# Linear attention with a feed-forward layer on one core: two loads moved to GpSimd's queue with a cast, the second weight in two pieces, and a new order of the work

## The chip, the cores and the metric

The kernel runs on one core of one Trainium2 chip. A core has five engines that run side by side, each through its own list of instructions: TensorE (PE, matrix products; PEld is its weight load), VectorE (DVE), ScalarE (ACT), GpSimd (POOL) and SyncE (SP), which here only issues transfers. Sixteen DMA engines move data between the main memory and the on-chip memory SBUF; the results of matmuls lie in the eight banks of PSUM. The metric is the device time of one execution in microseconds, as the median of several runs.

## The reference

For each of 4 batches and 8 heads, over 768 steps of 48 channels, a state of 48 x 48 is decayed and updated, and read by q:

```python
f = 1.0 / (1.0 + np.exp(-f_logit))
for t in range(S):
    state = f[:, :, t, :, None] * state + np.einsum('bhd,bhe->bhde', k[:, :, t], v[:, :, t])
    y[:, :, t] = np.einsum('bhd,bhde->bhe', q[:, :, t], state)
```

The heads of y are laid side by side, which gives 3072 tokens of 384 channels. A feed-forward layer follows:

```python
h = x @ w_in                       # 384 -> 2048
g = h * (1.0 / (1.0 + np.exp(-h)))
return g @ w_out                   # 2048 -> 384
```

All inputs and the output are float32; w_in and w_out have 3.1 MB each.

## The kernel before

The 768 steps of each batch are cut into six chunks of 128. A chunk of one batch, with its eight heads, is a "unit of work"; two of them form a pair, and there are twelve pairs (lines 19 to 32). Pairs 0 to 3 have the form T: they hold the chunks 0 and 1 of one batch, and the 128 partitions hold two neighbouring steps each, so that one load of 384 KB brings the f (or k, q, v) of both chunks in runs of 384 bytes. Pairs 4 to 11 have the form N: the same chunk of two batches, mostly in two loads of 192 KB.

A step of the work has a short name and the pair's number, and for most kinds the half of the pair (0 or 1):

- `f`, `k`, `q`, `v`: the loads (lines 224 to 241), all on SP's queue before the change.
- `E`, `L`: ACT turns f_logit into the log of the decay (exp, then ln). `cs`: PE sums it over time by a product with a triangular matrix. `ia`, `a`: ACT takes the exponential of the sum, with both signs; `al`: the decay over a whole half.
- `ki`, `qg`: k and q times these factors, on DVE or POOL (line 341). `tq`: PE transposes both, `qkc` copies them out of PSUM; for later pairs a transposing transfer `qkD` does both.
- `sc`: the scores of one half against the other operand, `at`: DVE masks them. `sc` of a T pair reads the transposed tiles of both halves.
- `vb`: v is cast to bfloat16 by ACT, DVE or POOL (line 343).
- `y`, `yi`: the output from the scores and from the state before. `d`, `sd`, `su`: the update of the state.
- `yc`, `yT`, `xc` (or `yD`): the output is cast and transposed into the input of the feed-forward layer.
- `wi`, `wo`: the loads of w_in and w_out, issued by POOL and cast to bfloat16 by the transfer (lines 209 to 219). Before, each comes in four pieces. `wi.n` holds the columns of `mi` blocks 2n and 2n + 1; a piece `wo.n` holds rows of w_out.
- `mi`: one block of 256 of the 2048 hidden channels (line 271). For pairs 0 and 1 it is cut once more by the half of the pair, so that `mi.0.4.1` is pair 0, block 4, half 1, of six matmuls. `si`: the sigmoid-weighted step on ACT (line 276). `mo`: a quarter of the product with w_out (line 306, four matmuls); `mo.P.i.n` uses rows 4n to 4n + 3 of sixteen blocks of rows. `oc`: the copy of the result out of PSUM. `so`: its store.
- `idle.512.n`: n matmuls of 512 columns on a tile of zeros (line 465), whose result nobody reads.

The order is written out by hand, as it were: the string `PLAN` (line 37) is a list of words `step:engine:buffers`. `f.2.0:S:1` is the load of f for pair 2, issued by S (SP), into buffer 1 of its class; A, V, G, P are ACT, DVE, POOL and PE. `SLOTS` (line 34) says how many buffers a class has. The kernel walks through the words (lines 510 to 516) and gives each step to its engine, so that each engine executes its own steps in the order of the words, and waits at a step until its inputs are there and its buffer is free. An engine never skips a step that waits. Ahead of everything else stand the first four loads of the list (line 482), then some constants are built. `count` (line 174) finds into how many pieces a load is cut from the number of words that name it, and `cast` (line 177) holds the pairs whose v is issued by G: such a load goes into a bfloat16 tile `vq` (lines 227 and 228), and `values` (line 199) then reads that tile where it otherwise reads `vb`. The code for this is there before the change; the plan before does not use it.

Two waits are named in the steps of the prediction. `y.0` writes into PSUM buffers that earlier `cs` tiles held, and can start when `ia` and `a` have read them. POOL's steps between the weight loads (`ki.3.0`, `qg.2.1`, `qg.3.0`, `qg.3.1`, `vb.3.0`) wait for loads on SP's queue.

Of the kernel before, what the change touches and what calls it, by code (L numbers as in the profile page):

```python
# [33 lines left out]
SLOTS = dict(f=4, k=6, q=6, v=6, e=2, lf=3, x=5, qk=5, vb=7, qkT=4, qkTT=2, atm=4, yb=3, xT=4, hT=4, sd=2, al=6, ob=6, pb=8, st0=1, st1=1, st2=1, st3=1)  # L34
# [15 lines left out]
mi.1.1.0:P:0 mi.1.4.0:P: qg.3.0:V: mi.1.1.1:P: si.1.4:A: mi.1.6.1:P:4 v.4.1:S:4 si.0.5:A: mi.0.1.1:P:6 mi.1.0.0:P:3 si.1.1:A: mi.1.3.1:P:5 mi.0.0.1:P:  # L50
mi.0.1.0:P: si.0.0:A: mi.1.0.1:P: si.0.3:A: mi.0.7.0:P:0 mi.0.6.1:P:7 mi.1.3.0:P: mi.1.7.0:P:1 si.1.3:A: mi.0.6.0:P: si.0.1:A: mi.1.7.1:P: mi.1.6.0:P:
tq.3.0:P:5 si.1.6:A: mo.0.0.0:P:6 si.1.7:A: si.0.6:A: tq.3.1:P:4 si.0.4:A: mi.0.7.1:P: qkc.3.1:V:1 mo.0.0.1:P: si.1.0:A: qkc.3.0:V: si.0.7:A:
mo.0.1.0:P:1 vb.2.1:G:4 vb.3.1:A:5 mo.0.1.1:P: vb.3.0:A:6 vb.2.0:G:2 sc.3.1:P:7,2 sc.3.0:P:4,3 at.3.1.0:V:2 f.5.0:S:1 mo.0.1.2:P: at.3.0.1:V:3
mo.1.1.0:P:5 q.5.1:S:4 at.3.0.0:V: mo.1.1.1:P: mo.1.1.2:P: E.4.0:A:0 v.4.0:S: mo.1.1.3:P: mo.0.1.3:P: v.8.1:S:5 mo.0.0.2:P: oc.0.1:V:0 k.4.1:S:4
at.3.1.1:V: y.2:P:0,7 oc.1.1:V:1 v.5.0:S:0 d.2:P:3,4 yc.2.0:A:0 d.3:P:1,2 su.2.0:V:0 so.1.1:G: y.3:P:5,0 yc.3.0:V:2 yi.2.1:P: yT.2.0:P:3 yc.2.1:A:1
mo.0.0.3:P: su.1.1:G:0 L.4.0:A:1 mo.1.0.0:P:5 oc.0.0:V:2 q.6.0:S:5 xc.2.0:A:2 su.3.0:V:0 yT.2.1:P:7 so.0.0:G: yT.3.0:P:6 cs.4.1:P:3 sd.2.1:V:1
mo.1.0.1:P: a.4.1:A:3 q.4.1:S:0 xc.2.1:V: E.5.0:A:1 cs.4.0:P:1 mi.2.7:P:4 k.5.1:S:5 ia.4.1:A:0 ia.4.0:A:2 mi.2.5:P:7 ki.4.1:G:3 k.4.0:S: al.4.0:A:4
al.4.1:A:5 L.5.0:A:2 mo.1.0.2:P: su.2.1:G:0 a.4.0:A:4 yi.3.1:P: mi.2.1:P:3 yc.3.1:V:0 q.4.0:S: mi.2.6:P:1 f.6.0:S:2 yT.3.1:P:0 mo.1.0.3:P: xc.3.1:V:3
xc.3.0:V: v.5.1:S: sd.3.1:V:0 mi.2.3:P:0 qg.4.1:V: mi.3.3:P:6 si.2.3:A:2 si.2.1:A: mi.2.4:P:2 si.2.7:A: mi.2.0:P:0 si.2.6:A: mi.3.5:P:3 si.2.0:A:
qkD.4.1:S:0 si.2.5:A: mi.3.1:P:4 si.3.5:A:3 mi.3.2:P:1 si.3.3:A: mi.3.6:P:0 vb.4.1:A:3 k.5.0:S: mi.2.2:P:7 si.3.6:A: q.5.0:S: si.2.4:A: vb.5.1:G:0  # L60
mo.2.0.0:P:3 f.7.0:S:3 si.2.2:A: mo.2.1.0:P:6 si.3.1:A: mi.3.4:P:0 si.3.2:A: v.7.0:S:1 mi.3.7:P:2 si.3.4:A: mi.3.0:P:7 k.6.1:S:0 mo.2.0.1:P: si.3.0:A:
# [48 lines left out]
def kernel(  # L110
# [436 lines left out]
```

## Time and profile before

| | |
|---|---|
| median of 3 runs | 181.59 us (181.53 to 183.5) |
| the profiled execution | 182.17 us, span 180.3 us |
| PE busy | 171.2 us, 95% of the span |
| PE weight load busy | 129.3 us, 72% |
| ACT busy | 129.0 us, 72% |
| DVE busy | 82.5 us, 46% |
| POOL busy | 63.4 us, 35% |
| SP's queue | 25.60 MB, 71.2% of the DMA engines' time |
| POOL's queue | 6.00 MB, 16.1% |
| mean granted clock of PE | 0.991 |

The span is the part of the execution that the profile covers, from the first instruction to the last; the execution's own time has some 1.9 us around it. Busy time of PE includes the `idle` matmuls, 8.3 us for 25 of them. The queue q1 is SP's, q0 is POOL's. A row of the timeline gives the start, the duration, the engine, the line and the operation, its output and input, how many instructions are merged, and in brackets how long the engine had been idle and what ended that.

### The profile page before, as it was taken

The numbers are of one execution on the slowest core, as the hardware profiler recorded it, in microseconds if no ns is written. First come the engines' busy times: TensorE is split into PE (matmuls) and PEld (weight loads), VectorE is DVE, ScalarE is ACT, GpSimd is POOL, SyncE is SP. The second block draws the span as 40 slices with busy tenths as digits, with TensorE's granted clock in tenths as the row PEclk, the third lists the DMA queues.
The fourth block names the chain that finished last, engine by engine and source line by source line (L and its number), as shares of the span: only waits on it lengthen the run. The fifth ranks groups of instructions, "written<-read, shape, count | busy, mean of one in ns | idle before, by whom it ended". The sixth has DMA issues, their size and how long they took to land.

```text
span 180.3 us, 4983 instructions
## 1 busy us (share of the span) xinstructions
PE 171.2 (95%) x2045; PEld 129.3 (72%) x2045; DVE 82.5 (46%) x170; ACT 129.0 (72%) x242; POOL 63.4 (35%) x111
## 2 busy tenths in 40 slices
PE   6579999999999999999999999999999999999993
PEld 2237688985778876778679777876776786788692
DVE  6046986124644029775595743167116865200012
ACT  4788787685486989697987579998197895548500
POOL 6027965502344102950488361054034361200001
PEclk9978999999999999999999999999999999999999
DMA  5999999999999999999959898995895889340023
GB/s 117 306 279 279 224 221 206 205 199 192 204 239 190 199 193 194 167 171 197 167 111 160 208 268 128 209 222 128 167 230 134 165 210 171 125 119 0 0 69 110
DMA packets 109366, 31.91 MB, mean 177 GB/s; under 512 B 103536, under 2 KB 108768, under 8 KB 109344
## 3 DMA queue, kind: packets, MB, share of 16 engines
q1 hardware_dynamic: 104464, 25.60, 71.2%
q0 software_dynamic: 4880, 6.00, 16.1%
q8 instruction: 16, 0.26, 0.6%
q14 instruction: 6, 0.05, 0.1%
HBM read 25.17 MB, written 4.72 MB: 166 GB/s over the span
## 4 chain that ended last, share of the span: by engine, by line
PE 77%; DMA 8%; ACT 5%; POOL 4%; DVE 2%; issue 1%; SPq 1%; ACTq 0%
PE pb L306 34%; PE pb L271 31%; DMA w_in_sb<-in_moe_w_in_dram 5%; DMA f<-in_f_logit_dram 3%; PE pb L373 2%; PE pb L385 2%; POOL qk L341 2%; PE pb L389 2%; ACT hT L276 2%; PE pb L348 1%; PE pb L331 1%; POOL w_in_sb L216 1%; PE pb L406 1%; ACT lf L260 1%; DVE ob L187 1%
## 5 line engine op out<-in xcount | busy, mean ns | idle before, releaser
L306 PE MATMUL pb<-w_out_sb,hT 128*128 128x384 bf16 (+1 forms) x416 | 70.5, 314 | 0.0
L271 PE MATMUL pb<-xT,w_in_sb 128*128 128x256 bf16 (+1 forms) x672 | 68.5, 257 | 0.2
L276 ACT ACTIVATE hT<-pb 128x512 bf16<-128x512 f32 x96 | 51.0, 607 | 19.2 <-PE pb L271 18.9
L271 PEld LDWEIGHTS <-w_in_sb 128*128 128x128 bf16 x672 | 56.7, 97 | 7.6 <-DMA w_in_sb<-in_moe_w_in_dram 0.3
L306 PEld LDWEIGHTS <-hT 128*128 128x128 bf16 x416 | 37.7, 97 | 18.0
L377 DVE TENSOR_TENSOR atm<-pb,triu 128x512 bf16<-128x512 f32 x32 | 20.6, 684 | 28.0 <-PE pb L373 23.9
L336 ACT ACTIVATE x<-pb 128x384 f32<-128x384 f32 x48 | 21.7, 496 | 3.2 <-POOL qk L341 1.9
L420 POOL TENSOR_TENSOR st<-sd,al 48x192 bf16<-48x192 f32 x32 | 17.0, 532 | 15.3 <-PE pb L385 13.7
L187 DVE COPY ob<-pb 128x384 f32<-128x384 f32 (+1 forms) x16 | 8.5, 529 | 27.4 <-PE pb L306 27.4
L513 ACT ACT_TABLE_LOAD x15 | 19.2, 1283 | 0.2
L187 POOL CAST vb<-v 128x384 bf16<-128x384 f32 x12 | 6.5, 552 | 32.4 <-DMA v<-in_v_dram 32.3
L341 POOL TENSOR_TENSOR qk<-k,x 128x384 bf16<-128x384 f32 x9 | 9.3, 1037 | 22.2 <-ACT x L336 13.7
L248 ACT ACTIVATE e<-f 128x768 f32<-128x768 f32 (+1 forms) x13 | 10.4, 799 | 7.2 <-DMA f<-in_f_logit_dram 7.1
L318 POOL DMA_DIRECT2D out_dram<-ob x8 | 4.5, 566 | 28.7 <-DVE ob L187 19.9
L341 POOL TENSOR_TENSOR qk<-q,x 128x384 bf16<-128x384 f32 x10 | 10.3, 1027 | 10.0 <-ACT x L336 5.6
L185 ACT CAST yb<-pb 128x384 bf16<-128x384 f32 x15 | 7.1, 483 | 6.9 <-PE pb L389 3.6
L377 DVE TENSOR_TENSOR atm<-pb,mask 128x512 bf16<-128x512 f32 x16 | 10.2, 683 | 3.3 <-PE pb L369 3.3
L341 DVE TENSOR_TENSOR qk<-k,x 128x384 bf16<-128x384 f32 x15 | 9.8, 667 | 4.1 <-ACT x L336 2.2
L410 DVE TENSOR_TENSOR sd<-pb,st 128x384 f32<-128x384 f32 x16 | 8.8, 552 | 5.9 <-PE pb L406 3.0
L185 ACT COPY ob<-pb 128x384 f32<-128x384 f32 (+1 forms) x10 | 4.6, 458 | 9.3 <-PE pb L306 9.3
L341 DVE TENSOR_TENSOR qk<-q,x 128x384 bf16<-128x384 f32 x14 | 9.3, 667 | 1.7 <-DMA q<-in_q_dram 1.2
L465 PE MATMUL pb<-zero,triu 128*128 128x512 bf16 x25 | 8.3, 471 | 1.4 <-POOL triu masks.py:66 1.4
(71 smaller groups left out, 155.7 us busy)
## 6 DMA issues: line engine op xcount, KB each, us to landing
f<-in_f_logit_dram SPq DMA_DIRECT2D x11, 384.0 KB, 4.9
v<-in_v_dram SPq DMA_DIRECT2D x16, 192.0 KB, 4.0
q<-in_q_dram SPq DMA_DIRECT2D x16, 192.0 KB, 4.4
k<-in_k_dram SPq DMA_DIRECT2D x16, 192.0 KB, 3.9
q<-in_q_dram SPq DMA_DIRECT2D x4, 384.0 KB, 6.1
v<-in_v_dram SPq DMA_DIRECT2D x4, 384.0 KB, 12.3
k<-in_k_dram SPq DMA_DIRECT2D x4, 384.0 KB, 5.6
w_in_sb<-in_moe_w_in_dram POOLq DMA_DIRECT2D x4, 384.0 KB, 9.2
```

The lines of the kernel that those rows point to most:

```text
L185: nc.scalar.copy(dst, src)
L187: ENG[eng].tensor_copy(dst, src)
L248: return nc.scalar.activation(e, at("f", P)[:, j * w:(j + 1) * w], AF.Exp, scale=-1.0)
L271: nc.tensor.matmul(h[:, i, cols], w_in_sb[:, kk, n * 128:(n + 1) * 128], at("xT", P)[:, kk, cols], start=(kk == 0), stop=(kk == KT - 1))
L276: return nc.scalar.activation(at("hT", P)[:, 2 * j:2 * j + 2, :], at("h", P, j).rearrange("p (n c) -> p n c", n=2), AF.Silu)
L306: nc.tensor.matmul(at("o", P, i, *rest[3:])[:, cols], at("hT", P)[:, n, i * C:(i + 1) * C], w_out_sb[:, n, cols], start=(n == 0), stop=(n ...
L336: nc.scalar.activation(at(kind, P, i).rearrange("p h d -> p (h d)"), at("cs", P, i)[:, 0:HD], AF.Exp, scale=1.0 if kind == "ia" else -1.0)
L341: ENG[eng].tensor_mul(at("qk", P, i)[:, j, :, 0:D], heads("qk"[j], P, i), at("ia" if j else "a", P, i))
L377: ENG[eng].tensor_mul(at("atm", P, i)[:, r], at(f"s{r}", P, i).rearrange("p (n c) -> p n c", c=C), mask[:, None, :].to_broadcast([C, NP, C]))
L410: nc.vector.tensor_add(at("sd", P, i), d_ps, prev_state(P, i))
L420: ENG[eng].tensor_mul(at("st", P, i)[lo:lo + D, :, r * D:(r + 1) * D], src[lo:lo + D, :, r * D:(r + 1) * D], al_of(P, i)[lo:lo + D, :, Non ...
L513: nc.scalar.preload_act_table_set(TABLES[mode])
```

## The change

All of it is in `SLOTS` and `PLAN`; no function is edited.

- `v.0.0` and `v.1.0` are issued by G instead of S, with the new class `vq` of two buffers. Each becomes one transfer of 1,024 runs of 384 bytes that casts on its way; `vb.0.0`, `vb.0.1`, `vb.1.0` and `vb.1.1` are gone. The class `v` has five buffers instead of six.
- `wo` has two pieces instead of four, eight blocks of rows each, so that `wo.0` serves `mo.P.i.0` and `mo.P.i.1`, and `wo.1` the other two.
- The first loads on SP's queue are f.2.0, f.0.0, f.0.1, f.1.0 instead of f.0.1, f.0.0, f.2.0, f.1.0: the whole load of f.2 stands ahead of the two halves of f.0.
- The order of all steps is another one, and 76 steps are on another engine. Of stores, for example, POOL issues ten instead of fifteen and SP the others. The order of pairs 2 and 3 in the head is exchanged: k, q and the transposes of pair 3 come first. The `idle` blocks have 23 matmuls in seven places instead of 25 in six.

The number of PE's steps of each kind is the same but for `idle`. The first words of both plans, up to where pair 0's `mi` begin (the two are not aligned with each other):

```diff
-SLOTS = dict(f=4, k=6, q=6, v=6, e=2, lf=3, ..., pb=8, st0=1, st1=1, st2=1, st3=1)
+SLOTS = dict(f=4, k=6, q=6, v=5, e=2, lf=3, ..., pb=8, vq=2, st0=1, st1=1, st2=1, st3=1)
-f.0.1:S:0 f.0.0:S: f.2.0:S:1 f.1.0:S:2 q.0.0:S:0 E.0.1:A:0 E.0.0:A: v.1.0:S:0 L.0.0:A:0 L.0.1:A: E.2.0:A:1 k.0.0:S:0 idle.512.11::0 cs.0.0:P:0
-cs.0.1:P:1 L.2.0:A:1 k.1.0:S:1 a.0.0:A:0 cs.2.0:P:2 a.0.1:A:1 ia.0.0:A:2 q.1.0:S:1 cs.2.1:P:3 E.1.0:A:0 al.0:A:0 L.1.0:A:2 vb.1.0:V:0 f.3.0:S:3
...
+f.2.0:S:0 f.0.0:S:1 f.0.1:S: f.1.0:S:2 k.0.0:S:0 E.2.0:A:0 q.0.0:S:0 E.0.0:A:1 L.2.0:A:0 f.3.0:S:3 E.0.1:A: idle.512.12::0 cs.2.0:P:0 L.0.0:A:1
+L.0.1:A: k.1.0:S:1 idle.512.1::1 cs.0.0:P:1 cs.0.1:P:2 ia.0.0:A:0 q.1.0:S:1 E.1.0:A:0 ki.0.0:G:0 a.0.0:A:1 q.3.0:S:2 al.0:A:0 v.0.0:G:0 ia.0.1:A:2
+qg.0.0:V: L.1.0:A:2 idle.512.3::3 tq.0.0:P:3 k.3.0:S:2 ki.0.1:G:1 a.0.1:A:3 cs.1.0:P:4 cs.1.1:P:5 ia.1.0:A:4 qg.0.1:V: v.1.0:G:1 a.1.0:A:0 q.2.0:S:3
+qkc.0.0:V:0 a.1.1:A:1 idle.512.1::6 tq.0.1:P:6 ia.1.1:A:2 cs.2.1:P:7 E.3.0:A:1 qkc.0.1:V: qg.1.1:G:2 k.2.0:S:3 L.3.0:A:1 sc.0.0:P:1,2 ki.1.1:G:
+sc.0.1:P:4,3 at.0.0.0:V:0 al.2:A:1 al.1:A:2 cs.3.1:P:6 ki.1.0:V:3 wi.2:G: tq.1.1:P:5 at.0.1.1:V:1 wi.1:G: qkc.1.1:A:1 v.2.0:S:0 wi.0:G: qg.1.0:V:
+at.0.1.0:V: a.2.1:A:3 idle.512.3::1 tq.1.0:P:1 ia.3.1:A:1 cs.3.0:P:3 qkc.1.0:V: wi.3:G: al.3:A:3 ia.3.0:A:2 at.0.0.1:V: a.3.0:A:4 v.3.0:S:1 ki.3.0:G:4
+idle.512.2::5 sc.1.1:P:5,4 ia.2.1:A:0 sc.1.0:P:1,3 at.1.1.1:V:2 y.0:P:2,7 at.1.0.1:V:3 a.3.1:A:2 yc.0.0:A:0 at.1.0.0:V: d.0:P:4,6 d.1:P:3,2 qg.2.1:G:0
...
```

After the change the steps of the head stand in this order on three of the engines:

```
SP:   f.2.0 f.0.0 f.0.1 f.1.0 k.0.0 q.0.0 f.3.0 k.1.0 q.1.0 q.3.0 k.3.0 q.2.0 k.2.0 v.2.0 v.3.0 f.4.0
POOL: ki.0.0 v.0.0 ki.0.1 v.1.0 qg.1.1 ki.1.1 wi.2 wi.1 wi.0 wi.3 ki.3.0 qg.2.1 qg.3.0 qg.3.1 su.1.1 wo.0 qg.2.0 su.0.1 vb.3.0 wo.1
PE:   y.0 d.0 d.1 yT.0.0 yi.0.1 y.1 yT.0.1 mi.0.4.0 yi.1.1 tq.3.0 yT.1.0 yT.1.1 mi.0.5.0 mi.0.5.1 mi.0.4.1 mi.1.4.0
      mi.1.2.0 mi.1.3.1 mi.1.3.0 mi.1.5.1 mi.1.2.1 tq.3.1 mi.0.0.1 mi.0.0.0 mi.1.1.1 mi.1.1.0 mi.1.4.1 mi.1.5.0 sc.3.0
      tq.2.1 tq.2.0 mi.0.3.1 mi.0.7.1
```

Before it they stand so:

```
SP:   f.0.1 f.0.0 f.2.0 f.1.0 q.0.0 v.1.0 k.0.0 k.1.0 q.1.0 f.3.0 v.0.0 k.2.0 q.2.0 k.3.0 q.3.0 v.3.0 v.2.0 f.4.0
POOL: ki.0.0 qg.1.1 qg.1.0 wi.1 vb.1.1 wi.2 vb.0.0 ki.2.0 ki.2.1 wi.0 qg.2.0 wi.3 wo.0 wo.1 ki.3.0 wo.2 wo.3 qg.3.1 su.0.1 vb.2.1
```

128 lines of the change are left out of this document (61 added, 67 removed).

## The prediction

> **What bounds the kernel now.** I read the page first, for the span and for which engine is full.
>
> ```profile
> span 180.3 us, 4983 instructions
> PE 171.2 (95%) x2045; PEld 129.3 (72%) x2045; DVE 82.5 (46%) x170; ACT 129.0 (72%) x242; POOL 63.4 (35%) x111
> ```
>
> PE is full, no other engine is. An average over 180 us does not say where PE waits, so the span is cut at the places where its behaviour changes (columns: stretch and its length; busy us and instructions of PE, PEld, DVE, ACT, POOL; clock; DMA share; GB/s).
>
> ```profile
> 0.00:24.90 24.90, 19.50 (x289) 11.84 (x290) 14.75 (x48) 18.39 (x37) 14.15 (x32) 0.93 0.99 239
> 24.90:28.26 3.36, 2.93 (x71) 2.57 (x69) 1.57 (x4) 3.03 (x6) 1.94 (x3) 1.00 1.19 218
> 28.26:32.89 4.63, 4.53 (x83) 4.36 (x79) 3.51 (x6) 2.80 (x5) 1.72 (x3) 1.00 1.21 207
> ...
> 60.00:100.00 40.00, 39.97 (x463) 30.11 (x461) 23.48 (x43) 34.13 (x71) 18.32 (x30) 1.00 0.99 171
> ...
> 140.00:177.40 37.40, 37.34 (x373) 29.31 (x370) 11.76 (x19) 20.96 (x42) 6.56 (x11) 1.00 0.47 106
> ```
>
> From 28.3 us to 177.4 us PE has almost no gap, while the DMA share, about 1 until 100 us, falls to 0.47. Both plans hold the same PE steps (112 `mi`, 104 `mo`, 24 `cs`, 24 `sc`, 20 `y`, 16 `d`, and so on; only the dummy `idle` blocks differ). So an edit that frees ACT, DVE or POOL after 33 us buys nothing, and what counts is how much real PE work is done by a given moment of the head. The timeline shows what the head waits for.
>
> ```profile
> 6.61 0.84 ACT L248 ACTIVATE e<-f 128x768 f32<-128x768 f32 x1 [0.97 <-DMA f<-in_f_logit_dram]
> ...
> 10.20 0.36 DVE L187 CAST vb<-v 128x384 bf16<-128x384 f32 x1 [5.98 <-DMA v<-in_v_dram]
> ...
> 12.32 1.37 POOL L341 TENSOR_TENSOR qk<-k,x 128x384 bf16<-128x384 f32 x1 [8.40 <-DMA k<-in_k_dram]
> ...
> 14.71 1.00 POOL L341 TENSOR_TENSOR qk<-q,x 128x384 bf16<-128x384 f32 x1 [1.02 <-DMA q<-in_q_dram]
> ...
> 16.87 0.95 POOL L216 DMA_DIRECT2D w_in_sb<-in_moe_w_in_dram  x1
> ...
> 32.28 1.30 POOL L341 TENSOR_TENSOR qk<-q,x 128x384 bf16<-128x384 f32 x1 [2.91 <-DMA q<-in_q_dram]
> ...
> 32.89 0.78 PEld L271 LDWEIGHTS <-w_in_sb 128*128 128x128 bf16 x14 [0.27 <-DMA w_in_sb<-in_moe_w_in_dram]
> ```
>
> Nearly every wait is for a load. At 32.89 the last piece of w_in lands, and PE is there 0.27 us early with 17 half-width `mi`, two `tq` and two `sc` of pairs 2 and 3 behind it. That moment is my gauge.
>
> **How the loads share the engines.** A load of f, k, q or v of a T pair is 1,024 runs of 384 B; I call it a unit. DMA traffic in stretches, SP's queue (q1) and POOL's (q0); packets, MB, share of 16 engines: 12 to 16 us; 20 to 24 (two rows); 24 to 28; 28 to 32 (two rows); 36 to 40.
>
> ```profile
> q1 hardware_dynamic: 2850, 1.08, 102.9%
> ...
> q0 software_dynamic: 519, 0.52, 79.7%
> q1 hardware_dynamic: 796, 0.30, 35.0%
> ...
> q0 software_dynamic: 535, 0.53, 78.3%
> ...
> q0 software_dynamic: 626, 0.59, 87.1%
> q1 hardware_dynamic: 631, 0.24, 33.7%
> ...
> q0 software_dynamic: 741, 0.55, 88.1%
> ```
>
> SP alone serves 2,850 packets in 4 us: a unit takes 1.44 us, a packet 64/2850 = 22.5 ns of one of 16 engines. Beside the weights it falls to 796, then 631: 5 to 6.5 us a unit. The queues take turns, 1.5 SP packets to one of POOL's at first, one to one later, and a weight packet is long (0.797 x 64 / 519 = 98 ns for w_in, 0.881 x 64 / 741 = 76 ns for w_out). Hence a load that misses the start of the weights is late by several us. Issues of w_in, of w_out, then k.3 and v.3, each followed by its time to landing (min/median/max):
>
> ```profile
> L216 POOL DMA_DIRECT2D w_in_sb<-in_moe_w_in_dram x4: 779/790/946, 16.9 to 23.2; - x4
> ...
> DMA to landing us min/median/max: 7.5/9.2/9.7
> ...
> L219 POOL DMA_DIRECT2D w_out_sb<-in_moe_w_out_dram x4: 750/762/791, 24.0 to 28.6; - x4
> ...
> DMA to landing us min/median/max: 12.2/14.2/16.0
> ...
> L241 SPq DMA_DIRECT2D k<-in_k_dram x1: 1349/1349/1349, 16.2 to 16.2; - x1
> ...
> DMA to landing us min/median/max: 9.1/9.1/9.1
> ...
> L241 SPq DMA_DIRECT2D v<-in_v_dram x1: 2449/2449/2449, 18.8 to 18.8; - x1
> ...
> DMA to landing us min/median/max: 19.2/19.2/19.2
> ...
> q1 hardware_dynamic: 12876, 4.87, 93.9%
> ...
> q0 software_dynamic: 2, 0.00, 0.1%
> ```
>
> The pieces of w_in land from 24.4 to 32.9, one per 2.8 us; w_out's last at 44.6. The last two rows are the traffic of 0 to 19.8 us: by the first weight packets (2.9 us after their issue) SP has served 12.6 units. So k.3, the 13th, lands at 25.3, q.3, the 14th, at 32.2, v.3, the 15th, at 38.0.
>
> **The change part by part.** *f.2 first.* Two rows for the first two issues (the halves of f.0, together one unit) and one for an Exp of 384 columns:
>
> ```profile
> L241 SPq DMA_DIRECT2D f<-in_f_logit_dram x2: 458/473/488, 0.7 to 1.3; - x2
> ...
> DMA to landing us min/median/max: 2.7/2.8/2.9
> ...
> L336 ACT ACTIVATE x<-pb 128x384 f32<-128x384 f32 x48 | 21.7, 496 | 3.2 <-POOL qk L341 1.9 <-PE pb L331 0.8 <-PE pb L334 0.5
> ```
>
> The first unit lands at 1.3 + 2.9 = 4.2, the second at 6.6, the fifth at 10.2; so f.2 lands at 4.2, f.0's halves at 5.4 and 6.6, k.0 (now the fourth, without v.1 ahead of it) at 9.0 instead of 12.3, q.0 at 10.2. ACT, in its new order, with 0.84 for a whole E or L and 0.5 for a half: E.2 to 5.0, E.0.0 to 5.9, L.2, E.0.1, L.0.0, L.0.1 to 8.3; cs.0.0; ia.0.0 to 9.4 (0.5 us each for `ia` and `a`), E.1, a.0.0, al.0, ia.0.1 to 11.4, L.1, a.0.1, ia.1.0, a.1.0, a.1.1 to 14.2, ia.1.1 to 14.7, E.3, L.3 to 16.4. Behind it stand qkc.1.1 (about 1 us, done at 19.0) and six reads of the `cs` of pairs 2 and 3 to 21.65; the last, ia.2.1, frees the PSUM buffer 7 that y.0 takes. y.0 at 21.7, against about 20 now; then yc.0.0, d.0, d.1, yT.0.0, su.0.0, yi.0.1, y.1, yT.0.1, with 3.6 us of their own durations and hand-overs, and mi.0.4.0 could start at 25.3. The first `mi` now starts at about 25.0: the early f.2 and k.0 buy nothing, since f.0 comes later and ACT has the same work ahead of y.0.
>
> *v.0, v.1 by POOL.* Four casts go; the page prices POOL's:
>
> ```profile
> L187 POOL CAST vb<-v 128x384 bf16<-128x384 f32 x12 | 6.5, 552 | 32.4 <-DMA v<-in_v_dram 32.3
> ...
> L318 POOL DMA_DIRECT2D out_dram<-ob x8: 540/575/587, 106.0 to 176.1; - x8
> ```
>
> They lie beside load waits: worth 0. The issues stand on POOL before ki.0.1 and qg.1.1. ki.0.0 ends at 10.8 (9.4 and the 1.37 of the 12.32 row). A store of 128 runs costs 0.575, a w_out piece of 512 runs 0.762; 1,024 runs by that slope 1.0 us each (bounds 0.6 and 2). POOL: v.0 10.8 to 11.8, ki.0.1, v.1 12.9 to 13.9, qg.1.1 (q.1 lands at 14.6), ki.1.1 to 16.6, then the four w_in issues. They begin no later than now, but q0 is first in, first out, and v stands ahead. No row shows a 384 B run that is cast. Below, a plain packet's 22.5 ns; from the two kinds of weight packets (98 and 76 ns for 2,048 and 1,536 source bytes; 94 by the second q0 row) 26 to 37 ns. I take 30. Then 2 x 64 packets an engine take 3.84 us, and SP's 192 beside them (1.5 to one) 4.3 us: from 13.6 (10.8 + 2.9) to 21.8. In that time SP serves q.3, k.3 and q.2, so q.2 lands near 23; w_in starts **2.0 us later** than at 19.8 and lands from 26.4 to 34.9.
>
> *The order.* PE now: mi.0.4.0 at 26.4, yi.1.1, tq.3.0 (0.5), two yT (0.35), four `mi` of 0.35 (a chain row below: 84 matmuls in 4.86 us) to 29.2; wi.1 is there; five `mi`, tq.3.1 to 31.4; wi.0 at 32.1; six `mi`, sc.3.0, tq.2.1, tq.2.0 to 35.4; mi.0.3.1 to 35.75; wi.3 is there. Before its first use stand 17 half `mi` as before, two more `tq` and one `sc` less: 0.6 us more work. Loss: 35.75 - 32.89 - 0.6 = **2.25 us**.
>
> *w_out in two pieces.* The stretch from there to the first `mo` is 15 `mi`, two `sc` and d.2 (6.3 us): 42.0. wo.0 is issued by POOL at about 28 (behind qg.2.1 at 23 and three steps of 1 us), so it follows w_in without a gap and lands 5.9 us (half of 44.6 - 32.9) behind it: 40.8, hidden by 1.2. wo.1 stands on POOL behind vb.3.0, which waits for v.3; v.3 lands at about 40.8, when wo.0 leaves the engines. Issue 41.3, first packet 44.2, 5.9 us, landing lag 1.2: 51.3. mo.0.0.2 needs it 8.4 us after 42.0 (eight `mo` of 0.67, 3.2 us of small steps): 50.4. **0.9 us** of wait (bounds 0 and 3).
>
> ```profile
> 32.89 4.86 PE pb L271 x84
> ...
> 42.16 4.02 PE pb L306 x24
> ...
> 177.37 0.32 ACT L185 COPY ob<-pb 128x192 f32<-128x192 f32 x1 [3.96 <-PE pb L306]
> ```
>
> Other engine moves (vb, yc, oc, so) are covered by PE's full stretch; without that cover each costs its 0.5 us. ACT's table changes stay at 16. The end keeps its form, a half-width copy and a store on SP: 0, at worst 0.5.
>
> Sum: the profiled run took 182.17 (span 180.3 and 1.87 around it), 0.58 above the median 181.59. 182.17 + 2.25 + 0.9 = 185.3, on the median's scale **184.7**, 1.7% slower: within 2%, which is about what a measurement of this kernel tells from no change (178.0 to 185.2).
>
> **Rivals.** *One to one* (ends slower). If v's packets and SP's alternate, v is through at 20.3 (128 x 52.5 ns), SP has then served q.3 and k.3 only, and q.2 has 0.9 unit left under the weights: 20.3 + (25.3 - 19.8) + 0.4 x 6.9 = 28.6. POOL holds qg.2.1 ahead of qg.3.0, and tq.3.0 needs qg.3.0: 30.6, with all later `mi` behind it. PE then does 8.2 us of work to the gauge: 38.8, a loss of 5.3, and wo.1 is no longer waited for. 182.17 + 5.3 - 0.58 = 186.9. It decides from q.2 landing after 24.8, and exceeds 2% from 26.9. For it: the one-to-one rows of 28 to 32; against it 519 to 796. The Trainium skill, "DMA: Bandwidth & Descriptors", section "Queues, rings and completion order", has each engine go round the queues packet by packet, which would be this rival; the trace agrees from 28 us on, not before. If PE also idles long, the clock may fall, as it did here (0.66):
>
> ```profile
> 10.00:15.00 5.00, 3.88 (x31) 2.65 (x31) 2.41 (x5) 3.82 (x10) 1.66 (x2) 0.66 1.06 284
> ```
>
> 3.4 us at half speed cost 1.7: 188.6.
>
> *No queue cost* (a small gain). Cast packets cost 22.5 ns or less, w_in starts as now, q.2 slips in, wo.1 comes in time: the 0.6 us of extra work remain: 181.0. More than 2% would need 3.6 us; even if all 24 half `mi` that need no wi.3 stood ahead of it, instead of 17, that would be 2.5 us.
>
> *The casts mattered*: if four casts of 0.5 us had delayed PE, 2 us come back: 182.7. Against it: POOL sits 32.3 us on v's loads.
>
> **How the numbers follow.** Forecast 0.50 (its own range 183 to 186), one to one 0.30, with the clock 0.07, no queue cost 0.08, casts 0.05. Faster by 2% only by something unseen: 0.03. Slower by 2%: the second and third, 0.37, less 0.07 for q.2 landing between 24.8 and 26.9, and the upper part of the forecast's range, 0.12: 0.42. Within: 0.55. The range 181.5 to 188.0 leaves out the best gain and the clock.
>
> **What would show it.** The first w_in landing near 26.4 and the last near 34.9; qg.2.1's wait on POOL ending near 23 (forecast) or 28 (rival); the first `mi` at 26.4; a wait on w_out by a load of L306 near 50; PE full after that. A w_in landed by 33, or PE gaps after 60 us, would make me wrong.

## The result, and the profile after

Twenty runs of the changed kernel have a median of 183.44 us (181.95 to 190.14); twenty of the kernel before, on the same chip, 182.41 us (181.43 to 183.93). The ratio is 1.0073, 95% interval 1.0051 to 1.0094: slower by three quarters of a per cent, within the 2% that count as no change. The forecast was 1.7% slower, within 2%, and the time lies in its range. But the traces show w_in early in every run of the new order, and no wait for wo.1 in the profiled run of the change: the two terms of its sum, a later w_in and that wait, are not what made this time there.

The ratio, like those below, leaves out executions that took over 1.5% more than the fastest of their kernel, and the profiled one (186.27 us) is such a one, because TensorE's clock was halved in two stretches of it; 13 of the 20 have no such stretch (mean clock 0.999 or more) and took 181.95 to 183.96. So its waits are read here for where they come from, not added up as the cost of the change.

The changed kernel's page, and the stretches shown of before (columns: stretch and length; busy us and instructions of PE, PEld, DVE, ACT, POOL; clock; DMA share; GB/s):

```profile
span 184.5 us, 4984 instructions
PE 172.5 (94%) x2043; PEld 131.2 (71%) x2043; DVE 80.4 (44%) x172; ACT 128.1 (69%) x241; POOL 57.9 (31%) x99
```

```profile
0.00:24.90 24.90, 18.65 (x281) 11.52 (x282) 15.01 (x47) 15.76 (x33) 12.69 (x29) 0.93 1.14 241
24.90:28.26 3.36, 1.28 (x24) 1.14 (x22) 0.50 (x2) 1.59 (x4) 3.19 (x4) 0.99 1.20 208
28.26:32.89 4.63, 4.63 (x58) 4.63 (x56) 0.62 (x2) 2.94 (x4) 2.72 (x4) 0.64 1.06 213
32.89:40.00 7.11, 7.11 (x146) 6.67 (x144) 4.61 (x9) 5.71 (x11) 2.84 (x4) 1.00 1.21 191
40.00:60.00 20.00, 19.93 (x295) 14.67 (x293) 9.05 (x20) 17.03 (x29) 4.93 (x8) 1.00 1.03 193
60.00:100.00 40.00, 40.00 (x437) 30.29 (x435) 20.67 (x42) 31.83 (x67) 13.18 (x21) 1.00 0.87 174
140.00:177.40 37.40, 37.24 (x362) 28.44 (x360) 11.21 (x21) 22.52 (x44) 4.09 (x7) 1.00 0.44 109
```

What bounds the kernel is what it was: from 28.3 us PE is full (0.07 us idle from 40 to 60, 0.16 from 140 to 177), and ACT, DVE and POOL have room. Nearly all of the difference between the two profiled runs is made in the head, up to 33 us. The timeline there, with the wait of each row in brackets:

```profile
19.39 0.98 POOL L340 TENSOR_TENSOR qk<-k,x 128x384 bf16<-128x384 f32 x1 [1.33 <-DMA k<-in_k_dram]
20.41 0.49 ACT L335 ACTIVATE x<-pb 128x384 f32<-128x384 f32 x1 [1.53 <-POOL qk L340]
20.95 1.16 PE L296 MATMUL pb<-vq,qk 64*128 64x96 bf16 x31 [1.42 <-ACT x L335]
...
25.07 3.08 POOL L340 TENSOR_TENSOR qk<-q,x 128x384 bf16<-128x384 f32 x3 [4.70 <-DVE xT L186]
26.28 0.49 ACT L335 ACTIVATE x<-pb 128x384 f32<-128x384 f32 x1 [2.53 <-POOL qk L340]
...
27.26 0.62 PE L347 MATMUL pb<-ident,qk 128*128 128x128 bf16 x8 [2.08 <-POOL qk L340]
```

Two waits of PE, each a chain that starts at a load. In the first, ki.3.0 on POOL waits for k.3; it holds the `x` buffer that a.3.1 on ACT writes next; a.3.1 reads the PSUM buffer 6 that d.0 takes; PE stands 1.42 us. In the second, qg.2.1 on POOL waits, qg.3.0 is queued behind it, and tq.3.0 needs qg.3.0: PE stands 2.08 us. The row names DVE as the releaser of qg.2.1, but DVE's copy had nothing to do with pair 2's q; what came at that moment is q.2's load. The issues of q.3 with k.3, then of k.3 with q.2, each pair followed by its least, middle and longest time to landing; then those of v.3 and of the last two pieces of w_in:

```profile
L240 SPq DMA_DIRECT2D q<-in_q_dram x1: 1327/1327/1327, 9.2 to 9.2; - x1
L240 SPq DMA_DIRECT2D k<-in_k_dram x1: 1149/1149/1149, 10.6 to 10.6; - x1
DMA to landing us min/median/max: 6.9/7.7/8.6
...
L240 SPq DMA_DIRECT2D k<-in_k_dram x1: 1149/1149/1149, 10.6 to 10.6; - x1
L240 SPq DMA_DIRECT2D q<-in_q_dram x1: 2393/2393/2393, 11.8 to 11.8; - x1
DMA to landing us min/median/max: 8.6/10.9/13.1
...
L240 SPq DMA_DIRECT2D v<-in_v_dram x1: 6402/6402/6402, 21.0 to 21.0; - x1
DMA to landing us min/median/max: 12.4/12.4/12.4
...
L215 POOL DMA_DIRECT2D w_in_sb<-in_moe_w_in_dram x2: 760/761/762, 16.5 to 17.3; - x2
DMA to landing us min/median/max: 11.7/12.6/13.5
```

k.3 lands at 10.6 + 8.6 = 19.2, q.2 at 11.8 + 13.1 = 24.9, v.3 at 33.4, and the last piece of w_in at 17.3 + 13.5 = 30.8, 2 us earlier than before (32.9) and not 2 us later, as forecast.

The clock is halved twice, 0.4 and 0.9 us after PE resumes from these waits. The two stretches, then 54 half-width `mi` by the chain of the changed kernel:

```profile
21.40:24.80 3.40, 3.40 (x67) 2.70 (x64) 2.80 (x7) 0.86 (x2) 0.00 (x0) 0.50 1.20 207
28.20:31.60 3.40, 3.40 (x36) 3.40 (x34) 0.62 (x2) 3.00 (x4) 2.78 (x4) 0.50 1.10 236
...
28.21 4.64 PE pb L270 x54
```

The same 54 matmuls at full clock, in the chain of the kernel of the first experiment below:

```profile
27.49 3.02 PE pb L270 x54
```

So the second stretch cost 1.6 us. The profiled run's arithmetic: PE is not busy for 184.5 - 172.5 = 12.0 us, against 180.3 - 171.2 = 9.1 before (1.4 and 2.1 are the two waits, before had smaller ones; 0.36 more lies behind PE's last matmul), and it is busy 1.3 us longer for the same matmuls less two dummies, at half the clock for 6.8 us (before, 3.4 us). That is the 4.2 us by which the two spans differ.

### The profile page after: what moved, and what is told of

It reads as the page before. It is cut to its first block, busy times and chain, and to the rows that moved or that the text cites. A ratio compares the mean times of both kernels' runs of the same rounds, so it can differ in the third digit from the quotient of the medians.

```text
span 184.5 us, 4984 instructions
## 1 busy us (share of the span) xinstructions
PE 172.5 (94%) x2043; PEld 131.2 (71%) x2043; DVE 80.4 (44%) x172; ACT 128.1 (69%) x241; POOL 57.9 (31%) x99
## 4 chain that ended last, share of the span: by engine, by line
PE 83%; SPq 5%; DMA 5%; issue 2%; ACT 1%; POOL 1%; DVE 1%; POOLq 0%; DVEq 0%
PE pb L270 34%; PE pb L305 34%; SPq L240 5%; DMA k<-in_k_dram 5%; PE pb L372 3%; PE pb L384 2%; PE pb L388 2%; PE pb L347 2%; PE pb L330 1%; PE pb L396 1%; POOL qk L340 1%; PE pb L405 1%; ACT hT L275 1%; PE pb L296 1%; PE pb L368 1%
## 5 line engine op out<-in xcount | busy, mean ns | idle before, releaser
L270 PE MATMUL pb<-xT,w_in_sb 128*128 128x256 bf16 (+1 forms) x672 | 70.6, 262 | 0.2 <-ACT hT L275 0.2
L275 ACT ACTIVATE hT<-pb 128x512 bf16<-128x512 f32 x96 | 51.5, 605 | 25.2 <-PE pb L270 24.8
L270 PEld LDWEIGHTS <-w_in_sb 128*128 128x128 bf16 x672 | 58.8, 101 | 7.7 <-DMA xT<-yb 0.4
L419 POOL TENSOR_TENSOR st<-sd,al 48x192 bf16<-48x192 f32 x32 | 17.2, 539 | 36.2 <-PE pb L384 24.0
L512 ACT ACT_TABLE_LOAD x15 | 19.2, 1283 | 0.3
L186 DVE COPY ob<-pb 128x384 f32<-128x384 f32 (+1 forms) x14 | 7.0, 509 | 20.7 <-PE pb L305 20.7
L317 POOL DMA_DIRECT2D out_dram<-ob x5 | 2.9, 573 | 39.3 <-ACT ob L184 32.9
L340 POOL TENSOR_TENSOR qk<-q,x 128x384 bf16<-128x384 f32 x11 | 11.1, 1012 | 5.6 <-DVE xT L186 4.7
L340 DVE TENSOR_TENSOR qk<-q,x 128x384 bf16<-128x384 f32 x13 | 7.5, 576 | 9.7 <-ACT x L335 9.7
L340 DVE TENSOR_TENSOR qk<-k,x 128x384 bf16<-128x384 f32 x15 | 9.1, 617 | 2.9 <-ACT x L335 2.9
L186 DVE COPY xT<-pb 128x384 bf16<-128x384 bf16 x7 | 2.4, 357 | 17.0 <-PE pb L396 14.5
L184 ACT COPY ob<-pb 128x384 f32<-128x384 f32 (+1 forms) x12 | 5.8, 480 | 5.2 <-PE pb L305 5.2
L347 PE MATMUL pb<-ident,qk 128*128 128x128 bf16 x80 | 6.0, 220 | 3.4 <-POOL qk L340 2.1
```

What stands on the lines that cost most here:

```text
L184: nc.scalar.copy(dst, src)
L186: ENG[eng].tensor_copy(dst, src)
L270: nc.tensor.matmul(h[:, i, cols], w_in_sb[:, kk, n * 128:(n + 1) * 128], at("xT", P)[:, kk, cols], start=(kk == 0), stop=(kk == KT - 1))
L275: return nc.scalar.activation(at("hT", P)[:, 2 * j:2 * j + 2, :], at("h", P, j).rearrange("p (n c) -> p n c", n=2), AF.Silu)
L340: ENG[eng].tensor_mul(at("qk", P, i)[:, j, :, 0:D], heads("qk"[j], P, i), at("ia" if j else "a", P, i))
L347: nc.tensor.transpose(t_ps[:, j, p, :], at("qk", P, i)[:, j, 2 * p:2 * p + 2, :], ident)
```

## The experiments

Each ratio is to runs of the kernel before beside it on the same chip; e11_late_nocast has none, its six executions differ too much for one. "First mo" is the start of the first `mo`, the end of the head.

| run | what | ratio (95%) | k.3 / q.2 / last w_in land | first mo |
|---|---|---|---|---|
| e12_f2_first | before, f.2 first | 1.0005 (0.9972 to 1.0038) | 26.9 / 20.1 / 32.7 | 37.9 |
| e3_cast_alone | before, v.0 and v.1 cast by the load | 1.0038 (1.0003 to 1.0074) | 19.1 / 17.7 / 31.6 | 37.1 |
| e4_wo2_alone | before, w_out in two pieces | 1.0088 (1.0055 to 1.0121) | 27.3 / 20.0 / 33.3 | 39.1 |
| the change | all, and the new order | 1.0073 (1.0051 to 1.0094) | 19.2 / 24.9 / 30.8 | 43.4 |
| e5_undo_cast | the change, without the cast | 1.0068 (1.0031 to 1.0106) | 16.8 / 20.3 / 30.1 | 38.8 |
| e8_v0_only | the change, v.0 alone by the cast | 1.0064 (1.0027 to 1.0101) | 17.2 / 23.0 / 31.1 | 40.0 |
| e1_q2_behind | the change, qg.2.1 behind pair 3 | 1.0118 (1.007 to 1.0165) | 20.5 / 26.5 / 31.8 | 41.1 |
| e2_filler | the change, dummies ahead of tq.3.0 | 1.0117 (1.008 to 1.0155) | 18.5 / 21.0 / 31.7 | 41.0 |
| e7_k3_first | the change, k.3 ahead of q.3 | 1.0106 (1.0079 to 1.0133) | 15.4 / 20.6 / 31.1 | 38.7 |
| e6_both | e1 and e7 together | 1.0059 (1.0033 to 1.0085) | 16.5 / 20.7 / 32.0 | 39.6 |
| e10_late | the change, three late edits | 1.0186 (1.0155 to 1.0218) | 18.4 / 20.7 / 31.7 | 39.2 |
| e9_late_k3 | e10 and e7 together | 1.0182 (1.0148 to 1.0216) | 16.2 / 23.3 / 31.8 | 40.3 |
| e11_late_nocast | e10 without the cast | none: 183.8 to 193.0 us | 16.6 / 20.1 / 30.2 | 38.6 |

The last two columns are of one profiled run each (before: 25.3 / 20.9 / 32.9, first mo 38.0). The second experiment's dummies and stretches of halved clock are in them.

**The two waits in the head.** The first theory was that q.2's chain, and the halved clock behind it, are the loss.

```diff
-qg.2.1:G:0 ... qg.3.0:G: ... qg.3.1:G:1      ia.2.0:A:3 ahead of yc.1.0
+qg.3.0:G: ... qg.3.1:G:1 qg.2.1:G:0          ia.2.0:A:3 behind qkc.3.0
```

> The changed kernel, but POOL does qg.2.1 (which waits for the load q.2) behind qg.3.0 and qg.3.1 instead of ahead of them, and ACT does ia.2.0, which needs a buffer that qg.2.1 frees, behind yc.1.0, yc.1.1 and qkc.3.0. Theory A (the changed kernel loses by tq.3.0, which stands on PE behind qg.3.0, so behind qg.2.1, so behind q.2's landing at 25 us, and by the half-speed clock that follows the gap): the gap of 2.1 us ahead of tq.3.0 falls below 0.5 us, no half-speed stretch lies after 28 us, and the time falls by 1.5 to 2 us, from 183.4 to about 181.7. Theory B (the loss is that v's packets stand ahead of the weights on POOL's queue): nothing of that moves, 183.4.

The wait goes, the time does not: 184.16 us, where 181.7 was expected. In that kernel's timeline PE no longer stands ahead of tq.3.0, though q.2 lands even later (26.5), so the chain was read rightly; but k.3 comes at 20.5 and the other wait has grown:

```profile
20.63 0.98 POOL L340 TENSOR_TENSOR qk<-k,x 128x384 bf16<-128x384 f32 x1 [2.00 <-DMA k<-in_k_dram]
21.65 0.49 ACT L335 ACTIVATE x<-pb 128x384 f32<-128x384 f32 x1 [2.21 <-POOL qk L340]
22.19 0.87 PE L296 MATMUL pb<-vq,qk 64*128 64x96 bf16 x31 [2.10 <-ACT x L335]
```

Dummies in the gap, to keep the clock up:

```diff
+idle.512.8::3 tq.3.0:P:3
```

> The changed kernel with 8 dummy matmuls of 512 columns on PE right ahead of tq.3.0. They fill the gap and end before tq.3.0 can start. Theory A: the wait for q.2 stays, but the clock stays at full speed from 28 us on, which is worth 1.5 us in the executions that had a half-speed stretch there (6 of 20) and nothing in the others: median 183.0, and no execution above 184.5. If the half-speed stretch has nothing to do with the gap, as many executions as before have a mean clock of 0.991 or less and the time stays at 183.4.

In its profiled run q.2 landed at 21.0 by itself, so there was no gap to fill and the dummies were 1.7 us of pure cost. The expectation failed: the median is 183.79 and not 183.0, the longest execution took 186.81, and 6 of 12 have a mean clock of 0.991 or less (7 of 20 without the dummies). The dummies did not keep the clock up; as the gap itself comes and goes, that decides nothing on what lowers it. It does show, as the table's column does, that under one order of the head q.2 lands anywhere from 20.7 to 26.5 us.

Then both waits together, and k.3's alone:

```diff
-q.1.0:S:1 ... q.3.0:S:2 ... k.3.0:S:2 ... q.2.0:S:3
+q.1.0:S:1 ... k.3.0:S:2 q.3.0:S:2 ... q.2.0:S:3
```

> The changed kernel with both late loads taken off PE's path: k.3 issued ahead of q.3 on SP, and qg.2.1 on POOL (ia.2.0 on ACT) behind the steps of pair 3. Theory B, the loss is two waits for loads that share the DMA engines with the cast v packets: k.3 lands near 17.5 instead of 19.2, PE's gap ahead of d.0 is under 0.5 us (1.42 in the changed kernel), no gap ahead of tq.3.0 (2.08 there), the first mo starts near 39 (43.35 there, about 40.4 without its two half-speed stretches), fewer runs with a half-speed stretch; time about 182.0. Theory C, the loss lies in the rest of the new order, behind 40 us: time about 183.4, as the changed kernel.

> The changed kernel with k.3 issued ahead of q.3 on SP, nothing else. Theory B: PE's gap ahead of d.0 goes (1.42 to under 0.5), the one ahead of tq.3.0 stays near 2, because q.2's place on SP is the same; it eats most of what was gained: about 183.0. Theory C: about 183.4 with the gap ahead of d.0 gone all the same.

With both off the path the wait ahead of d.0 is 0.49 us, there is none ahead of tq.3.0, no clock is lost in the profiled run, the first `mo` starts at 39.6, and the time is 183.15: 1.2 us over the 182.0 forecast, and hardly under the changed kernel. With k.3 alone the head is the best of those with both casts in the changed order (first `mo` at 38.7, 0.25 us of wait ahead of d.0, and none ahead of tq.3.0, where about 2 was expected to stay), and the time is 183.84 instead of 183.0. So the head's two waits explain the profiled run and not the median. The timeline of that kernel shows what became of the head's gain; PE's two longest waits after 20 us, POOL's cast ahead of them, and the issue of wo.1 with its time to landing:

```profile
38.03 0.51 POOL L186 CAST vb<-v 128x384 bf16<-128x384 f32 x1 [6.59 <-DMA v<-in_v_dram]
...
48.41 0.81 PE L305 MATMUL pb<-w_out_sb,hT 128*128 128x384 bf16 x4 [1.17 <-DMA w_out_sb<-in_moe_w_out_dram]
...
161.47 1.70 PE L270 MATMUL pb<-xT,w_in_sb 128*128 128x256 bf16 x14 [0.73 <-DMA xT<-yb]
...
L218 POOL DMA_DIRECT2D w_out_sb<-in_moe_w_out_dram x1: 932/932/932, 38.5 to 38.5; - x1
DMA to landing us min/median/max: 9.9/9.9/9.9
```

vb.3.0 waits for v.3 (37.9), wo.1 is issued behind it at 38.5 and lands at 48.4, and PE, there early, stands 1.17 us: the prediction's w_out term, with its mechanism and nearly its size. At 161 us mi.11.7 waits for the transposing DMA of yD.11.1, with six `mi` ahead of it as cover. In the profiled run of the change neither bites (v.3 landed at 33.4, wo.1 at 45.0, PE was late). A late head hides them; a good one meets them.

**Half the dose.**

```diff
-v.1.0:G:1
+v.1.0:S:4 ... vb.1.0:G:2 vb.1.1:G:3    (behind ki.3.0)
```

> The changed kernel with half the dose: v.0 cast by its load on POOL's queue, v.1 by SP in its place (behind k.3) and cast by POOL. Theory B: 64 cast packets an engine fewer beside SP's loads; k.3 lands near 18, q.2 near 22.5 (24.9 with both on POOL's queue, 20.3 with none), no gap ahead of tq.3.0; time about 182.3. A load that waits on the engines in full either way (one queue or two, the same bytes) would leave q.2 near 25 and the time at 183.4.

q.2 at 23.0 instead of 22.5, but still 1.61 us of wait ahead of tq.3.0 and hardly a change of the ratio (1.0064). The dates of q.2 (20.3 with no cast, 23.0 with one, 24.9 with two) go with the dose, but the other runs' 20.7 to 26.5 with two are as wide: the dose isn't shown in them.

**The parts by themselves, in the old order.**

```diff
-f.0.1:S:0 f.0.0:S: f.2.0:S:1 ... E.0.1:A:0 E.0.0:A: ... E.2.0:A:1
+f.2.0:S:0 f.0.1:S:1 f.0.0:S: ... E.2.0:A:0 E.0.1:A:1 E.0.0:A:
```

> The kernel before with f.2 loaded ahead of f.0's halves and its Exp first on ACT, nothing else. The prediction's step: worth 0, as f.0 lands 1.4 us later and ACT has the same work: same time as before within 0.3 us. Rival: f.0's delay of 1.4 us reaches the first ki and w_in's issues: about 1 us slower.

Nothing, as the prediction had it. In this pair of traces the load stream is a little quicker with a whole load first. The issue of q.0, which is the fourth unit in both, in this kernel, with its time to landing:

```profile
L241 SPq DMA_DIRECT2D q<-in_q_dram x1: 1151/1151/1151, 3.1 to 3.1; - x1
DMA to landing us min/median/max: 5.0/5.0/5.0
```

and in the kernel before:

```profile
L241 SPq DMA_DIRECT2D q<-in_q_dram x1: 1686/1686/1686, 3.0 to 3.0; - x1
DMA to landing us min/median/max: 6.0/6.0/6.0
```

The cast alone:

```diff
-v.1.0:S:0 ... v.0.0:S:1 ... vb.0.0 vb.0.1 vb.1.0 vb.1.1
+ki.0.0:G: v.0.0:G:0 ... qg.1.1:G:3 v.1.0:G:1
```

> The kernel before, with only v.0 and v.1 moved to POOL's queue with the cast (v.0 behind ki.0.0, v.1 behind qg.1.1) and their four casts taken out; five buffers for v instead of six. Theory B (my prediction's first term): v's packets push the first weight packet from 19.8 to about 21, the last piece of w_in from 32.9 to about 34, and the time rises by 1.2, to 183.6. Theory A: k.0 lands one unit earlier and q.3 before the weights, so PE's work ahead of the last piece of w_in is done in time, and the time is that of before within 0.5 us.

In the profiled run everything of the head comes about 1 us earlier (first `mo` 37.1 against 38.0), with q.2 ahead of k.3 and q.3 on SP in this order and landing at 17.7. Yet the time is 0.4% worse, at the edge of no change. The clock goes with it: 8 of its 12 executions have a halved stretch, 5 of 29 of the kernel before beside it; those without one have the same median in both, 181.50. Undone in the new order:

```diff
-v.0.0:G:0 ... v.1.0:G:1
+v.0.0:S:5 ... v.1.0:S:4 ... vb.0.0:G:0 vb.0.1:G:1 (behind wi.3) ... vb.1.0:G:2 vb.1.1:G:3 (behind ki.3.0)
```

> The changed kernel with v.0 and v.1 back on SP's queue, at the same places in the list, and their four casts on POOL behind the w_in issues (v.0) and behind ki.3.0 (v.1); six buffers for v, none for vq. Theory B: the weights start 1.5 us earlier, the last piece of w_in lands near 29.3 instead of 30.8, and the time falls by up to 1.5, to 182. Theory A: q.2 is now the 13th load on SP's queue instead of the 11th and again finishes under the weights, near 24.5 us, tq.3.0 waits as long as before, and the time stays at 183.4 within 0.5.

The ratio is the change's 0.7%, but it is made in another way. Of its 12 executions 9 have a halved stretch, and the other three took 181.77 to 182.05, against 181.50 of the kernel before. The changed kernel takes 183.10 in the middle of its 13 without one. So the ratio alone does not say that the loss lies outside the cast: without the cast there is less loss at full clock, and more of the halved clock.

w_out in two pieces alone:

```diff
-wo.0:G: ... wo.1:G: ... wo.2:G: ... wo.3:G:     (a quarter each)
+wo.0:G: ... wo.1:G:                             (a half each)
```

> The kernel before with w_out in two pieces instead of four, nothing else. By the prediction's term the second piece is not held by v.3 here, so no wait for it. The first piece lands where the second of four does now, 39.0, and the first mo starts at 38.04: a wait of about 1 us at most, on the path: 181.6 to 182.6. If pieces' sizes do not matter at all: 181.6.

0.9% slower, more than the 1 us allowed at most, and here a cause stands in PE's timeline (of an execution of 185.41 us, one of the longer; the median is 184.04):

```profile
39.14 0.82 PE L306 MATMUL pb<-w_out_sb,hT 128*128 128x384 bf16 x4 [0.45 <-DMA w_out_sb<-in_moe_w_out_dram]
...
44.97 4.71 PE L306 MATMUL pb<-w_out_sb,hT 128*128 128x384 bf16 x28 [1.71 <-DMA w_out_sb<-in_moe_w_out_dram]
```

The bytes end at the same time (44.9 against 44.6), but the third quarter, there at 41.9 before, is now part of a half that is not there until 44.9. In the old order a half's granularity costs 0.45 + 1.71 us of waits in this run. PE also waits 0.64 and 1.10 us for pieces of w_in in it, but so it does in e12_f2_first (0.54 and 1.10), which is no slower than before.

**The late losses.** The last theory was that the head's gains are given back at wo.1, at mi.11.7 and in the end of the kernel.

```diff
-vb.3.0:G:2 ... wo.1:G:           mo.9.1.3 ... mo.9.0.3 ... y.11.1 mi.10.4 mi.10.5 mi.10.7     so.11.1.0:S:
+wo.1:G: vb.3.0:G:2               y.11.1 mi.10.4 mi.10.5 mo.9.1.3 mi.10.7 mo.9.0.3             so.11.1.0:G:
```

> The changed kernel with its three late losses taken away and its head left: wo.1 issued on POOL ahead of vb.3.0, two mo of pair 9 moved behind y.11.1 to give pair 11's transposing DMA time, so.11.1.0 issued by POOL. Theory D, the rest of the loss lies behind the head, where whatever the head gains is given back: at the wait for wo.1 (1.17 us in the run with k.3 first), at mi.11.7's wait for its transpose (0.16 to 0.94 in all runs of the new order), and 0.36 at the end. Then: no PE gap at 48 us, none near 161, end of PE to end of span 3.0 instead of 3.33, time 0.5 to 1 us under the changed kernel's: about 182.4. Theory B, head alone: 183.1 or more, because nothing of the head is touched.

> The same with k.3 issued ahead of q.3. Theory D: the 2.3 us that the run with k.3 first lost behind its head (1.17, 0.8 and 0.36) come back: 183.8 less 2.3, about 181.5, level with the kernel before or under it. Theory B: 183.8 less nothing, or 183.0.

> The same three late edits with v.0 and v.1 on SP and their casts on POOL, k.3 where the changed kernel has it. If the cast by the load is worth nothing or harms in the new order: about 181.2, as e5 without a half-speed stretch (181.8) less its late losses of 0.6. If it helps: above the run with k.3 first and the late edits.

e10_late is 1.1% slower than the change, e9_late_k3 0.8% slower than with k.3 first alone, and the profiled span of e11_late_nocast is 182.1 us against 180.3 of e5_undo_cast. The wait for wo.1 is gone and another has taken its place. Timeline and chain of e10_late:

```profile
43.66 0.84 ACT L247 ACTIVATE e<-f 128x768 f32<-128x768 f32 x1 [2.15 <-DMA f<-in_f_logit_dram]
...
45.80 0.39 PE L396 MATMUL pb<-ident,yb 128*128 128x128 bf16 x3 [1.70 <-ACT yb L184]
...
21.24 22.39 DMA f<-in_f_logit_dram
```

wo.1's packets, issued at 31.7 instead of 36.7 on POOL's queue, share the engines with SP's, and f.4 lands at 43.6 instead of 39.3. E.4 on ACT waits for it; yc.2.0 stands behind E.4 and L.4 on ACT, and yT.2.0 on PE needs it: 1.70 us (1.6 to 1.7 in all three). The end became longer too, 3.77 us behind the last matmul instead of 3.33. So the theory that the late waits can be had back is not borne out. Until 45 us the loads of both queues compete for the DMA engines, and in these runs moving a load only moved the wait. In e11_late_nocast five of six executions have a halved stretch as well. No version here is under the kernel before.

What stays open: how the 0.7% of the median divides. The parts by themselves come to 0 + 0.4 + 0.9%, each with its interval, and the new order then has taken back 0.6 of it, or the parts overlap; the runs do not tell. A part of it is the clock, which the ratios mix in. The executions without a halved stretch (mean clock 0.997 or more) alone, with their median, and that of the kernel before beside them:

| run | without a halved stretch | median | before |
|---|---|---|---|
| e3_cast_alone | 4 of 12 | 181.50 | 181.50 |
| e5_undo_cast | 3 of 12 | 181.78 | 181.50 |
| e8_v0_only | 5 of 12 | 182.64 | 182.01 |
| e6_both | 7 of 8 | 183.12 | 182.01 |
| e4_wo2_alone | 6 of 10 | 183.94 | 182.01 |
| the change | 13 of 20 | 183.10 | not on record |

By these, w_out in two pieces is the costliest part by itself, the cast costs nothing in the old order, and in the new order the loss goes with the number of casts (none, one, two: 0.3, 0.6 and 1.1 us, the last without the head's two waits). That is a hint and no proof, with three to seven executions each, on two chips. Why k.3 and q.2 land up to 6 us apart from run to run was not found.

## Why the prediction was right or wrong

**What bounds it: right.** PE is full from 28 us in both; no ACT, DVE or POOL edit behind that shows.

**f.2 first costs nothing: right** (1.0005). Two dates behind it were late: k.0 was forecast to land at 9.0 and landed at 8.1, ki.0.0 took 1.00 us and not 1.37, and y.0 came at 18.9 instead of 21.7.

**The casts are worth 0, a POOL issue 1.0 us: right, as far as is shown.** In the old order the cast alone changes nothing at full clock (181.50 and 181.50); in the new order undoing it leaves the ratio, but not what the ratio is made of. The two issues took 0.93 and 1.09 us, starting at 9.5 and 11.6 instead of 10.8 and 12.9:

```profile
L227 POOL DMA_DIRECT2D vq<-in_v_dram x2: 932/1010/1089, 9.5 to 11.6; - x2
DMA to landing us min/median/max: 7.3/8.0/8.7
L215 POOL DMA_DIRECT2D w_in_sb<-in_moe_w_in_dram x4: 760/761/792, 15.0 to 17.3; - x4
DMA to landing us min/median/max: 8.0/10.7/13.5
```

**w_in 2.0 us later, a loss of 2.25: wrong, the step that failed.** It put the end of ki.1.1, and so the four w_in issues, at 16.6; they began at 15.0. The dates of the loads had been taken from the kernel before, which served 7,210 packets on SP in its first 12 us, while the changed one served 8,097. And it let v's packets hold w_in back until 21.8. The trace has w_in's first packet at 18.3, against 19.7 before; in e5_undo_cast, where no v stands ahead of it on that queue, it is at 18.3 too. In the other runs of the new order with both casts it is at 18.5 to 19.8. So the cast packets hold w_in up by 1.5 us at most, and never past the 19.8 of before; its last piece landed at 30.1 to 32.0 in every run of the new order, before the old 32.9: the prediction's own sign against itself ("A w_in landed by 33").

What was wrong there is the price of a packet. The changed kernel from 13 to 18 us and in the one microsecond from 14, e7_k3_first from 16 to 18, and the changed kernel again from 20 to 24; packets, MB and share of 16 engines:

```profile
q1 hardware_dynamic: 2029, 0.77, 62.7%
q0 software_dynamic: 2015, 0.38, 89.4%
...
q0 software_dynamic: 649, 0.12, 144.0%
q1 hardware_dynamic: 197, 0.07, 33.2%
...
q1 hardware_dynamic: 707, 0.27, 69.3%
q0 software_dynamic: 701, 0.13, 77.1%
...
q0 software_dynamic: 621, 0.61, 89.5%
q1 hardware_dynamic: 560, 0.22, 30.1%
```

A cast packet of 384 B lasts 0.894 x 80 us / 2015 = 35 ns, inside the bounds of 26 to 37. But the shares of the two queues add up to 152% in this stretch: packets overlap on an engine, so durations cannot be added up as the forecast did. A count avoids that. Alone, from 9 to 12 us, SP begins 856 packets in a microsecond, 18.7 ns of an engine for each, and not the 22.5 taken. What its 2,029 packets leave of the 80 us from 13 to 18 is, as an estimate, 21 ns for a cast packet; in e7_k3_first (2,405 and 2,021 packets from 13 to 19) it is 25.

**1.5 to one: wrong, and with it q.2's date.** Beside v's cast packets the turns are not fixed: 649 to 197 in favour of POOL's queue in one microsecond of the changed kernel, one to one in e7_k3_first from 16 to 18. Beside the weights it is one to one: 621 stand beside 560, and 595 beside 594 from 24 to 28. The rival had v's packets and SP's alternate, 52.5 ns for each two; in the changed kernel 2,000 of v's 2,048 had begun by 18 us, and not at 20.3. The Trainium skill's rule ("DMA: Bandwidth & Descriptors", section "Queues, rings and completion order"): each engine goes round the queues packet by packet, and a packet there is typically some 9 to 17 descriptors. The trace agrees in so far as the two queues take turns of one to one from 20 us on; it does not show what makes them unequal ahead of that. q.2 was forecast for 23 and landed at 24.9, a tenth past the 24.8 from which the rival decides, and its chain is in the profile link by link. But the rival's date was 28.6 and its price 5.3; the wait was 2.08. In other runs of the same head q.2 lands before 21 and the rival does not happen at all. The decision point was placed well; the date has a width of 6 us, and no single number was right for it.

**The half clock** was given 7 chances in 100, behind the long wait of the rival alone. It came behind waits of 1.4 and 2.1 us; its price, 1.7 a stretch, measured 1.6.

**wo.1's 0.9: the mechanism was right, the term right or 0 by the run.** It was 0 in the changed kernel's profiled run (v.3 landed 7 us before the forecast's 40.8), 1.17 in the run with k.3 first, and in the old order, without vb.3.0 ahead of it, 2.2, which the prediction did not look at: it asked when the second half is issued, and not what a half's granularity delays.

**The end: 0.36 us** (3.33 us from PE's last matmul to the end instead of 2.97), inside the bound "at worst 0.5". **Not foreseen:** k.3's chain through a.3.1 to d.0 (0.2 to 2.1 us), and mi.11.7's wait for a transposing DMA (up to 0.9).

So the sign and the class were right, but the larger term did not happen and the other one happened only in some runs; the 3.15 us of the sum stand against 1.3 measured (0.73% of 181.6). That the time lies in the range is luck as far as w_in goes: other losses, the head's waits for k.3 and q.2, the halved clock and, where the head is early, w_out's halves, fell in its place, and in what shares stays open.

## What to carry to other kernels

Where loads fill all DMA engines, give a load's date a width and not a value: work out from which date a wait decides, and list everything queued behind each waiting step, because the gain of one date is met by the next one. Ask of a load cut into fewer pieces when its first needed byte may be used, and not when its last byte lands. Before adding up durations of packets, see whether the shares of the queues add up to more than 1: then count packets in a stretch instead. And an experiment that takes a wait away has to be followed to the end of the span: here the wait for wo.1 came back as one for f.4, and a ratio stayed at 0.7% while what it was made of changed.

## What the hardware showed

The clock. Each halved stretch between matmuls of these traces is 3.4 us long and begins 0.1 to 0.9 us after PE resumes from a wait, and the waits were short: 1.3 us in the kernel before, 1.4 and 2.1 in the changed one, 2.1 in e1_q2_behind, 0.5 in e2_filler, 1.7 in e10_late. Others of 1.6 to 1.7 us (e8_v0_only, e4_wo2_alone, e11_late_nocast) were followed by none. Over the 3.4 us ahead of a stretch PE stood idle for 37 to 62% in sum. In the changed kernel the two stretches begin 6.8 us apart, twice 3.4. The Trainium skill, "TensorE: Matmul & The Clock Gate", section "HAM oscillation — how this bites in real kernels", gives as its rule that idle gaps of PE over about 3.4 us are to be avoided. In these traces much shorter ones are enough: gaps of 0.5 to 2.1 us came ahead of every halved stretch, though not every such gap was followed by one. What decides was not found.

A cast on the way. A packet of 384 B that lands as 192 is on record as lasting 35 ns, against 22.5 for a plain one of the same source, but the records overlap; by count it takes 21 to 25 ns of an engine (an estimate) against 18.7.

A whole load first. In the two pairs of rows above the fourth unit lands 0.9 us earlier when the first two issues are a whole load and a half instead of two halves; other traces of the old order have it at 8.6, so a part of it is scatter.
